# Prologue of an attention and SoLU-FFN kernel: fewer warming products, five paired key tiles, another order in the first score tile

## The chip, the cores and the metric

The kernel runs on one core of a Trainium2 chip. The metric is the device time of one execution in microseconds (us), as the median of several executions. TensorE (PE) multiplies matrices, VectorE (DVE), ScalarE (ACT) and GpSimd (POOL) work on the elements, and the queue of SyncE (SP) issues most of the DMAs.

## What is computed

Attention over pooled keys, and behind it a feed-forward layer with the SoLU activation, for 4 batches of 12288 tokens with 128 channels:

```python
r = 4
kv_pool = kv.reshape(B, H // r, r, W // r, r, C).mean(axis=(2, 4))
kv_flat = kv_pool.reshape(B, -1, C) @ w_sr        # 768 keys of 128 channels; k = v = kv_flat
s = (q @ k.transpose(0, 2, 1)) / sqrt(C)
a = softmax(s)                                     # written out: max, exp, sum
x = a @ v
h = x @ w_in                                       # 128 -> 1024
solu = h * softmax(h)
ln = (solu - mean) / sqrt(var + 1e-06) * g_ln
out = ln @ w_out                                   # 1024 -> 128
```

The weights of the feed-forward layer come as 64-bit floats and are taken apart into 32-bit parts on the chip.

## The kernel before

Work goes in tiles of 128 tokens, 384 tiles in all. A loop of slots is software-pipelined: in each slot one tile's scores `s` are made (L590, six products of 128x384), an earlier tile's values `xa`, hidden layer `h` and output `o`. All four engines are near full in it. The order of every instruction is written out by hand; each engine takes its own instructions strictly in that order, and waits on semaphores between engines.

The change lies in the prologue, ahead of the loop. The pooled keys of batch 0 are made there from 16 tiles `kv_0` (`kv_first_load`, L184): 8 tiles `c` for each half of the keys, each of 128 x 2 x 384 floats (384 KB). `kv_first` multiplies both planes of a tile with `w_sr16` on TensorE in float32 (two instructions for one product) and adds the products up in `pk`, one `pk` for each half. For the tiles named in `PAIRS` `kv_pair` first adds the second plane to the first, so that one product is enough; the tiles of half 1 are multiplied in the order `TURN1`. The tiles are called "tile 0" to "tile 7" of their half below. Out of `pk` come `kwh` (ACT, L211) and the remainder `kwl` (DVE, L214), 384 columns for each half; the first score tile `s_0` needs both halves of both, and of the queries `qwh` (ACT) and `qwl` (`q_low`, POOL, L573). The loop begins with `s_0`: its row maximum `nm` (DVE, L611), the exponential (ACT), and so on.

Beside that, the prologue takes the weights apart. `out_steps` are the seven steps for `w_out` on DVE, of which step 5 is a two-input operation over 128x1024 (`top_out`) and step 6 another (`rest_out`). POOL then subtracts (`wf`, L955) and adds (`wo`, L956, which needs step 6). Ahead of all products stand `WARM` products of a constant (L910), which nothing reads.

SP's queue issues all loads of the prologue in order: `w_sr`, `raw_in`, six tiles of half 0, `raw_out`, two tiles of half 0, the queries, the eight tiles of half 1 in the order 0 to 7, more queries and the first six tiles of batch 1.

Of the kernel before, what the change touches and what calls it, by code (L numbers as in the profile page):

```python
# [18 lines left out]
ALU = mybir.AluOpType  # L19
# [30 lines left out]
LOW_DVE = [NT - 2]  # L50
ROOM = {NT - 9: (0, 0), NT - 8: (0, 1), NT - 7: (0, 2), NT - 3: (1, 0), NT - 2: (1, 1), NT - 1: (1, 2)}

PAIRS = (2, 5, 6)
TURN1 = (0, 1, 3, 2, 4, 5, 7, 6)
OUT_AT = 6
Q_AT = 8
WARM = 20

Z_LEAST = 0.5
FIT_LEAST = 32.0  # L60
# [8 lines left out]
def kernel(  # L69
# [15 lines left out]
    nc = tc.nc  # L85
# [22 lines left out]
    def float64_parts(raw, name):  # L108


        pair = raw.rearrange("p (f two) -> p f two", two=2)
        lo, hi = pair[:, :, 0], pair[:, :, 1]
        top = wrk.tile([P, DFF], F32, tag="u", name=f"top_{name}", bufs=5)
        if name == "in":
            rest = wrk.tile([P, DFF], F32, tag="u", name="rest_in", bufs=5)
        else:
            rest = bat.tile([P, 2 * NK], F32, tag="acc", name="rest_out", bufs=1)[:, :DFF]
        ex = wrk.tile([P, DFF], I32, tag="e", name=f"ex_{name}")
        sgn = wrk.tile([P, DFF], I32, tag="e", name=f"sgn_{name}")
        scalar = nc.vector.tensor_scalar  # L120
        both = nc.vector.tensor_tensor
        and_, shr = ALU.bitwise_and, ALU.logical_shift_right
        return top, rest, [
            partial(scalar, ex, hi, 20, 0x7FF, op0=shr, op1=and_),
            partial(scalar, ex, ex, -896.0, 0.0, op0=ALU.add, op1=ALU.max),
            partial(scalar, ex, ex, 255.0, 2.0**23, op0=ALU.min, op1=ALU.mult),
            partial(
                nc.vector.scalar_tensor_tensor,
                ex,
                hi,  # L130
                -0x80000000,
                ex,
                op0=and_,
                op1=ALU.bitwise_or,
            ),
            partial(scalar, sgn, hi, 0xFFFFF, 3, op0=and_, op1=ALU.logical_shift_left),
            partial(both, top.bitcast(I32), ex, sgn, op=ALU.bitwise_or),
            partial(
                nc.vector.scalar_tensor_tensor,
                rest,  # L140
                lo.bitcast(U32),
                2.0**-52,
                ex.bitcast(F32),
                op0=ALU.mult,
                op1=ALU.mult,
            ),
        ]
# [36 lines left out]
        nc.sync.dma_start(t, kv0[:, 2 * c : 2 * c + 2, half * 384 : half * 384 + 384])  # L184
        state["kv0", half, c] = t

    def kv_pair(c):
        t = state["kv0", 1, c]
        nc.gpsimd.tensor_tensor(t[:, 0, :], t[:, 0, :], t[:, 1, :], op=ALU.add)

    def kv_first(half, c):


        if c == 0:
            state["pk0", half] = (ps_x, ps_r)[half].tile(
                [P, 512], F32, tag="xr"[half], name=f"pk_0_{half}"
            )
        t = state.pop(("kv0", half, c))
        n = 1 if half and c in PAIRS else 2
        last = TURN1[-1] if half else 7  # L200
        for r in range(n):
            nc.tensor.matmul(
                state["pk0", half][:, :384],
                w_sr16,
                t[:, r, :],
                start=c + r == 0,
                stop=c == last and r == n - 1,
            )
# [4 lines left out]
    def kv_first_l(half):  # L213
        nc.vector.scalar_tensor_tensor(  # L214
            half_of("kwl", 0, half),
            state["pk0", half][:, :384],
            SCALE,
            half_of("kwh", 0, half).bitcast(F32),
            op0=ALU.mult,
            op1=ALU.subtract,  # L220
        )
# [312 lines left out]
    def by_tile(a):  # L534
        return a.rearrange("p (t j) -> p j t", j=GT)

    def in_tiles(a):
        return a.rearrange("p (j t) -> p j t", j=GT)

    def wide(g):  # L540
        return g < GPB or g >= NG
# [9 lines left out]
    def q_split(g):  # L551
        if NG <= g < NG + GPB:
            return
        qf = state["qf", g // QL][:, (g % QL) * 512 : (g % QL + 1) * 512]
        if wide(g):
            qh = grp.tile([P, 512], F32R, tag="qwh", name=f"qwh_{g}")
            ql = grp.tile([P, 512], F32R, tag="qwl", name=f"qwl_{g}")
        else:
            qh = grp.tile([P, 512], F16, tag="qh", name=f"qh_{g}")
            ql = grp.tile([P, 512], F16, tag="ql", name=f"ql_{g}")  # L560
        if wide(g):
            nc.scalar.copy(in_tiles(qh), by_tile(qf))
        else:
            nc.scalar.copy(qh, qf)
        state["q", g] = (qh, ql)

    def q_low(g):
        if NG <= g < NG + GPB:
            return
        qf = state["qf", g // QL][:, (g % QL) * 512 : (g % QL + 1) * 512]  # L570
        qh, ql = state["q", g]
        if wide(g):
            nc.gpsimd.tensor_tensor(  # L573
                in_tiles(ql), by_tile(qf), in_tiles(qh.bitcast(F32)), op=ALU.subtract
            )
        else:
            nc.gpsimd.tensor_tensor(ql, qf, qh, op=ALU.subtract)


    def scores_pe(t):  # L580
        g, j = divmod(t, GT)
        b = t // TPB
        qh, ql = state["q", g]
        names = ("kwh", "kwl") if wide(g) else ("kh", "kl")
        kh, kl = (state[n, b] for n in names)
        tokens = in_tiles if wide(g) else by_tile
        s = ps_r.tile([P, 2, 512], F32, tag="r", name=f"s_{t}")
        for n, (lh, rh) in enumerate(((qh, kh), (qh, kl), (ql, kh))):
            for half in range(2):
                nc.tensor.matmul(  # L590
                    s[:, half, :384],
                    tokens(lh)[:, j, :],
                    rh[:, half * 384 : (half + 1) * 384],
                    start=n == 0,
                    stop=n == 2,
                )
        state["s", t] = s[:, :, :384]
        state["free"] = s[:, :, 384:]

# [308 lines left out]
    warm = ps_o.tile([P, 512], F32, tag="o", name="warm")  # L908
    for _ in range(WARM):
        nc.tensor.matmul(  # L910
# [3 lines left out]
            start=True,  # L914
            stop=True,
# [16 lines left out]
    wo, wor, out_steps = float64_parts(raw_out, "out")  # L932
# [2 lines left out]
        f()  # L935
    pow2_under(wsc)
    nc.vector.tensor_scalar(wsc, wsc, 2.0**14, None, op0=ALU.mult)
    for f in out_steps[2:]:
        f()
    q_split(0)  # L940
    q_low(0)
    nc.scalar.mul(wf, wf, wsc)
    nc.scalar.copy(w_in_h, wf)
    nc.scalar.mul(wr, wr, wsc)
# [3 lines left out]
    kv_first_t(0)  # L948
    kv_sq(0, 0)
    kv_first_l(0)  # L950
    for c in PAIRS:
        kv_pair(c)
    for c in TURN1:
        kv_first(1, c)
    nc.gpsimd.tensor_tensor(wf, wf, w_in_h, op=ALU.subtract)  # L955
# [121 lines left out]
    held = []  # L1077
    q_load(2)
    scores_pe(0)
    scores_pe(1)  # L1080
    for slot in range(NT):
        i = slot - LH
# [19 lines left out]
        if slot != 8:  # L1102
            at(slot + 2 if slot < 8 else slot + 1, scores_pe)
# [188 lines left out]
    n = nc.values_load(count[0:1, 0:1], min_val=0, max_val=P)  # L1292
# [37 lines left out]
```

## Time and profile before

| | us |
|---|---|
| median of 3 executions | 1843.61 |
| lowest and highest | 1842.31, 1850.59 |
| profiled execution | 1841.4 |
| its span, first to last instruction | 1839.5 |
| busy: PE, DVE, ACT, POOL | 1818.2, 1768.4, 1749.2, 1665.6 |

The profile is that of one execution. Its span is counted from the first instruction; 1.9 us lie around it. Rows give the start, the length and the instruction with what it writes and reads; brackets behind a row name the idle time ahead of it and what ended that. A row that stands for several instructions (x20) has their whole stretch. Starts overlap the instruction before by up to a tenth of a microsecond.

### The profile page before, as it was taken

Reading aid. Unit: us, or ns where it says so; the run is one execution under the profiler, and the core shown is the slowest. Engines: PE = TensorE matmul, PEld = TensorE weight load, DVE = VectorE, ACT = ScalarE, POOL = GpSimd, SP = SyncE. Lnnn points to the kernel's source line nnn. Section 1 sums busy time; section 2 is a strip of 40 time slices with the busy share of each in tenths; the row PEclk is TensorE's granted clock in tenths of the full one; section 3 lists DMA queues with packets and bytes.
Section 4 is the critical chain, followed back from the end, with each engine's and each line's share of the span. In section 5 each row is a group of like instructions: output and inputs, shape, how many; then the busy total and the mean of one; then the engine's idle time right before and its main releaser. Section 6 shows DMA issues by size and latency. Waiting matters only on the chain.

```text
span 1839.5 us, 42799 instructions
## 1 busy us (share of the span) xinstructions
PE 1818.2 (99%) x15747; PEld 1216.9 (66%) x15747; DVE 1768.4 (96%) x2635; ACT 1749.2 (95%) x3129; POOL 1665.6 (91%) x1466
## 2 busy tenths in 40 slices
PE   8999999999999999999999999999999999999998
PEld 5577777777666666566666666666666666666666
DVE  6999999999999999999999999999999999999997
ACT  5999999999999999899999999999999999999997
POOL 5899999899999999889999999998988988888887
PEclk9999999999999999999999999999999999999999
DMA  8999999999999999999999999999999999999998
GB/s 301 202 243 241 237 242 242 237 230 231 250 230 250 250 233 234 225 245 235 235 244 249 236 243 248 244 233 221 233 240 231 222 230 229 235 227 236 223 226 170
DMA packets 1440026, 432.79 MB, mean 235 GB/s; under 512 B 1404608, under 2 KB 1408832, under 8 KB 1439552
## 3 DMA queue, kind: packets, MB, share of 16 engines
q1 hardware_dynamic: 1433616, 413.45, 111.3%
q10 hardware_dynamic: 6192, 16.52, 3.5%
q8 instruction: 126, 2.06, 0.5%
q14 instruction: 92, 0.75, 0.1%
HBM read 52.50 MB, written 25.17 MB: 42 GB/s over the span
## 4 chain that ended last, share of the span: by engine, by line
PE 82%; ACT 8%; DVE 3%; DMA 2%; issue 2%; POOL 2%; SPq 0%; DVEq 0%; POOLq 0%; ACTq 0%
PE o L831 24%; PE h L703 23%; PE s L590 18%; PE xa L650 17%; ACT e L727 2%; ACT junk L806 2%; ACT phl L614 2%; ACT s L612 1%; DMA uT<-uhl 1%; DMA kv<-in_kv_dram 1%; POOL uhl L765 1%; DVE junkd L711 1%; DVE nm L611 1%; POOL uhl L758 1%; DVE phl L622 1%
## 5 line engine op out<-in xcount | busy, mean ns | idle before, releaser
L765 POOL TENSOR_TENSOR uhl<-u,uhl 128x1024 f16<-128x1024 f32 x382 | 814.5, 2133 | 31.7
L831 PEld LDWEIGHTS <-uT 128*128 128x128 f16 x9072 | 537.2, 98 | 95.9 <-DMA uT<-uhl 9.6
L831 PE MATMUL o<-wch,uT 128*128 128x128 f16 x6048 | 568.2, 219 | 5.0 <-DMA uT<-uhl 4.8
L831 PE MATMUL o<-wcl,uT 128*128 128x128 f16 x3024 | 526.1, 219 | 0.0
L741 DVE SCALAR_TENSOR_TENSOR u<-h,rz,e 128x1024 f32<-128x1024 f32 x384 | 491.1, 1279 | 26.4 <-ACT e L727 18.9
L711 DVE TENSOR_SCALAR_CACHE_REDUCE junkd<-h,rz 128x1024 bf16<-128x1024 f32 x384 | 490.7, 1278 | 1.5 <-PE h L703 1.1
L758 POOL TENSOR_SCALAR uhl<-u 128x1024 f16<-128x1024 f32 x379 | 395.8, 1044 | 84.7 <-DVE u L741 76.4
L650 PE MATMUL xa<-pT,vhl 128*128 128x512 f16 x1728 | 469.8, 380 | 0.0
L727 ACT ACTIVATE e<-h,nm,rz 128x1024 f32<-128x1024 f32 x384 | 458.5, 1194 | 3.0 <-DVE junkd L711 3.0
L806 ACT ACTIVATE junk<-u,su 128x1024 bf16<-128x1024 f32 x384 | 438.0, 1141 | 0.1
L611 DVE TENSOR_REDUCE nm<-s 128x1 f32<-128x768 f32 x384 | 363.9, 948 | 16.8 <-PE s L590 13.1
L612 ACT ACTIVATE s<-s,nm 128x768 f32<-128x768 f32 x384 | 335.0, 872 | 41.1 <-DVE nm L611 40.9
L622 DVE SCALAR_TENSOR_TENSOR phl<-s,phl 128x768 f16<-128x768 f32 x384 | 365.6, 952 | 2.9 <-ACT phl L614 2.9
L614 ACT ACTIVATE phl<-s 128x768 f16<-128x768 f32 x384 | 311.1, 810 | 12.2
L703 PEld LDWEIGHTS <-xh 128*128 128x128 f16 x1536 | 141.0, 97 | 194.5 <-DVE phl L622 32.3
L650 PEld LDWEIGHTS <-vhl 128*128 128x128 f16 x1728 | 162.5, 98 | 135.5 <-issue 12.8
L703 PE MATMUL h<-w_in_h,xh 128*128 128x512 f16 x768 | 229.1, 380 | 1.6 <-DVE rz L685 1.0
L703 PE MATMUL h<-w_in_h,xl 128*128 128x512 f16 x768 | 228.5, 379 | 0.0
L703 PE MATMUL h<-w_in_l,xh 128*128 128x512 f16 x768 | 228.5, 379 | 0.0
L590 PEld LDWEIGHTS <-qh 128*128 128x128 f16 x1152 | 124.2, 113 | 43.7 <-issue 0.7
L590 PE MATMUL s<-kh,qh 128*128 128x384 f16 x576 | 140.6, 326 | 0.6 <-DVE u L741 0.6
L590 PE MATMUL s<-kh,ql 128*128 128x384 f16 x576 | 140.9, 326 | 0.0
(153 smaller groups left out, 1816.8 us busy)
## 6 DMA issues: line engine op xcount, KB each, us to landing
qf<-in_q_dram SPq DMA_DIRECT2D x96, 256.0 KB, 3.6
out_dram<-ob SPq DMA_DIRECT2D x96, 256.0 KB, 2.7
kv<-in_kv_dram ACTq DMA_DIRECT2D x42, 384.0 KB, 4.4
kv<-in_kv_dram SPq DMA_DIRECT2D x22, 384.0 KB, 7.5
pT<-phl SPq DMA_TRANSPOSE x384, 4.0
uT<-uhl SPq DMA_TRANSPOSE x378, 4.5
raw_in<-in_moe_w_in_dram SPq DMA_DIRECT2D x1, 1024.0 KB, 5.0
raw_out<-in_moe_w_out_dram SPq DMA_DIRECT2D x1, 1024.0 KB, 9.8
```

The lines of the kernel that those rows point to most:

```text
L590: nc.tensor.matmul(s[:, half, :384], tokens(lh)[:, j, :], rh[:, half * 384 : (half + 1) * 384], start=n == 0, stop=n == 2,)
L611: nc.vector.tensor_reduce(nm, s, axis=AX.XY, op=ALU.max, negate=True)
L622: nc.vector.scalar_tensor_tensor(phl[:, 1], state.pop(("s", t)), SC, phl[:, 0], op0=ALU.mult, op1=ALU.subtract)
L650: nc.tensor.matmul(xa, v[:, c, :], pT[:, :, a * NKC + c, :], start=n == 0, stop=n == len(seq) - 1)
L703: nc.tensor.matmul(h[:, hs], lh[:, ts], rh[:, hs], start=n == 0, stop=n == 2)
L711: nc.vector.tensor_scalar(junk, state["h", t], state["rz", g][1][:, j : j + 1], None, op0=ALU.mult, op1=ALU.min, accum_out=nm,)
L727: nc.scalar.activation(e, state["h", t], AF.Exp, bias=nm, scale=state["rz", g][0][:, js], accum_out=state["z2", g][:, js],)
L741: nc.vector.scalar_tensor_tensor(u, state.pop(("h", t)), state["rz", g][2][:, j : j + 1], state.pop(("e", t)), op0=ALU.mult, op1=ALU.mult, ...
L758: nc.gpsimd.tensor_scalar(uhl[:, 0, :], u, 1.0, 1.0, op0=ALU.mult, op1=ALU.mult)
L765: low.tensor_tensor(uhl[:, 1, :], u, uhl[:, 0, :], op=ALU.subtract)
L806: nc.scalar.activation(junk, u, AF.Square, scale=-float(DFF), bias=su, accum_out=state["v3", g][:, j : j + 1],)
L831: nc.tensor.matmul(po[:, ts], uT[:, a * NFC + c, :], w[:, c, :], start=start, stop=stop)
```

## The change

`WARM` goes from 20 to 15. `PAIRS` goes from tiles 2, 5, 6 to tiles 2, 3, 4, 5, 6 of half 1, and `kv_pair` takes an engine: POOL adds tiles 2 and 5, DVE adds 3, 4 and 6. The additions are issued earlier: POOL's tile 2 ahead of `q_low`, tile 5 behind it; DVE's tile 3 ahead of step 5 of `out_steps`, tile 4 behind that step, and tile 6 behind the first half's `kwl`, followed by step 6. `TURN1` is new. The first score tile makes the three terms of half 0 first, and of half 1 the two that need only `kwh` ahead of the one that needs `kwl`. Nothing is loaded otherwise.

```diff
-PAIRS = (2, 5, 6)
-TURN1 = (0, 1, 3, 2, 4, 5, 7, 6)
+PAIRS = (2, 3, 4, 5, 6)
+TURN1 = (0, 1, 2, 3, 4, 6, 5, 7)
-WARM = 20
+WARM = 15
-    def kv_pair(c):
+    def kv_pair(c, eng):
         t = state["kv0", 1, c]
-        nc.gpsimd.tensor_tensor(t[:, 0, :], t[:, 0, :], t[:, 1, :], op=ALU.add)
+        eng.tensor_tensor(t[:, 0, :], t[:, 0, :], t[:, 1, :], op=ALU.add)
-        for n, (lh, rh) in enumerate(((qh, kh), (qh, kl), (ql, kh))):
-            for half in range(2):
+        order = [(n, half) for n in range(3) for half in range(2)]
+        if t == 0:
+            order = [(0, 0), (1, 0), (2, 0), (0, 1), (2, 1), (1, 1)]
+        for at, (n, half) in enumerate(order):
...
-    for f in out_steps[2:]:
+    for f in out_steps[2:5]:
         f()
     q_split(0)
+    kv_pair(2, nc.gpsimd)
     q_low(0)
+    kv_pair(5, nc.gpsimd)
+    kv_pair(3, nc.vector)
+    out_steps[5]()
+    kv_pair(4, nc.vector)
...
     kv_first_l(0)
-    for c in PAIRS:
-        kv_pair(c)
+    kv_pair(6, nc.vector)
+    out_steps[6]()
     for c in TURN1:
         kv_first(1, c)
```

On DVE, from the last single-input step of `out_steps` to the remainder of half 1. In the names `kv_3_148` is tile 3 of half 1, `pk_0` and `pk_1` are the sums of the two halves. Before:

```order
L939 TENSOR_SCALAR sgn_out<-raw_out 128x1024
L939 TENSOR_TENSOR top_out<-ex_out,sgn_out 128x1024
L939 SCALAR_TENSOR_TENSOR rest_out<-raw_out,ex_out 128x1024
L214 SCALAR_TENSOR_TENSOR kwl_120<-pk_0_206,kwh_119 128x384
L214 SCALAR_TENSOR_TENSOR kwl_120<-pk_1_257,kwh_119 128x384
```

And now:

```order
L943 TENSOR_SCALAR sgn_out<-raw_out 128x1024
L189 TENSOR_TENSOR kv_3_148<-kv_3_148 128x384
L949 TENSOR_TENSOR top_out<-ex_out,sgn_out 128x1024
L189 TENSOR_TENSOR kv_4_150<-kv_4_150 128x384
L214 SCALAR_TENSOR_TENSOR kwl_120<-pk_0_201,kwh_119 128x384
L189 TENSOR_TENSOR kv_6_154<-kv_6_154 128x384
L961 SCALAR_TENSOR_TENSOR rest_out<-raw_out,ex_out 128x1024
L214 SCALAR_TENSOR_TENSOR kwl_120<-pk_1_254,kwh_119 128x384
```

Three additions, each on a tile that must have landed, stand between the steps.

On POOL, from the power for `wsc` to the addition for `wo`. Before:

```order
L931 TENSOR_TENSOR wsc<-wsc,mhalf 128x1
L573 TENSOR_TENSOR qwl_236<-qf_140,qwh_235 128x512
L189 TENSOR_TENSOR kv_2_146<-kv_2_146 128x384
L189 TENSOR_TENSOR kv_5_152<-kv_5_152 128x384
L189 TENSOR_TENSOR kv_6_154<-kv_6_154 128x384
L955 TENSOR_TENSOR top_in<-top_in,w_in_h 128x1024
L956 TENSOR_TENSOR top_out<-top_out,rest_out 128x1024
```

And now:

```order
L935 TENSOR_TENSOR wsc<-wsc,mhalf 128x1
L189 TENSOR_TENSOR kv_2_146<-kv_2_146 128x384
L573 TENSOR_TENSOR qwl_229<-qf_140,qwh_228 128x512
L189 TENSOR_TENSOR kv_5_152<-kv_5_152 128x384
L964 TENSOR_TENSOR top_in<-top_in,w_in_h 128x1024
L965 TENSOR_TENSOR top_out<-top_out,rest_out 128x1024
```

Tile 6 is gone from POOL, and tile 2 stands ahead of `q_low`, so `q_low` now stands behind the landing of tile 2.

On PE, the products of half 1. Before:

```order
L202 MATMUL pk_1_257<-kv_0_142,w_sr_93 128x384 x2
L202 MATMUL pk_1_257<-kv_1_144,w_sr_93 128x384 x2
L202 MATMUL pk_1_257<-kv_3_148,w_sr_93 128x384 x2
L202 MATMUL pk_1_257<-kv_2_146,w_sr_93 128x384
L202 MATMUL pk_1_257<-kv_4_150,w_sr_93 128x384 x2
L202 MATMUL pk_1_257<-kv_5_152,w_sr_93 128x384
L202 MATMUL pk_1_257<-kv_7_156,w_sr_93 128x384 x2
L202 MATMUL pk_1_257<-kv_6_154,w_sr_93 128x384
```

And now:

```order
L202 MATMUL pk_1_254<-kv_0_142,w_sr_93 128x384 x2
L202 MATMUL pk_1_254<-kv_1_144,w_sr_93 128x384 x2
L202 MATMUL pk_1_254<-kv_2_146,w_sr_93 128x384
L202 MATMUL pk_1_254<-kv_3_148,w_sr_93 128x384
L202 MATMUL pk_1_254<-kv_4_150,w_sr_93 128x384
L202 MATMUL pk_1_254<-kv_6_154,w_sr_93 128x384
L202 MATMUL pk_1_254<-kv_5_152,w_sr_93 128x384
L202 MATMUL pk_1_254<-kv_7_156,w_sr_93 128x384 x2
```

Tiles 3 and 4 are down to one product, and tile 7, which lands last, closes the half.

## Rows read from the trace of the kernel before

**Rows 1.** The page's span and busy times: busy us (share of the span) xinstructions.

```profile
span 1839.5 us, 42799 instructions
PE 1818.2 (99%) x15747; PEld 1216.9 (66%) x15747; DVE 1768.4 (96%) x2635; ACT 1749.2 (95%) x3129; POOL 1665.6 (91%) x1466
```

**Rows 2.** PE's waits from 75 us on: us in total, times, longest; the largest.

```profile
PE o L831 <- DMA uT<-uhl: 4.8, 5, 2.1
```

**Rows 3.** The chain that ended last, first 36 us: start, length, what.

```profile
12.61 8.98 DMA kv<-in_kv_dram
...
21.64 6.17 PE pk L202 x18
...
27.82 0.50 ACT kwh L211
...
28.37 1.40 PE s L590 x5
...
29.79 0.97 DVE nm L611
```

**Rows 4.** PE's weight loads in order of time, one for each matmul instruction.

```profile
5.86 0.15 PEld L910 LDWEIGHTS <-ones 128*128 128x128 bf16 x1 [0.28 <-issue]
6.17 1.39 PEld L910 LDWEIGHTS <-ones 128*128 128x128 bf16 x7 [0.17 <-issue]
7.68 4.92 PEld L202 LDWEIGHTS pk<-kv,w_sr 128*128 128x128 f32 x16
...
16.04 2.23 PEld L202 LDWEIGHTS pk<-kv,w_sr 128*128 128x128 f32 x8 [0.42 <-DMA kv<-in_kv_dram]
18.66 2.23 PEld L202 LDWEIGHTS pk<-kv,w_sr 128*128 128x128 f32 x8 [0.39 <-DMA kv<-in_kv_dram]
21.64 0.94 PEld L202 LDWEIGHTS pk<-kv,w_sr 128*128 128x128 f32 x4 [0.74 <-DMA kv<-in_kv_dram]
22.75 1.76 PEld L202 LDWEIGHTS pk<-kv,w_sr 128*128 128x128 f32 x6 [0.17 <-POOL kv L189]
...
25.58 1.59 PEld L202 LDWEIGHTS pk<-kv,w_sr 128*128 128x128 f32 x6 [0.42 <-DMA kv<-in_kv_dram]
```

**Rows 5.** PE in order of time, behind its longest wait after the start.

```profile
33.75 0.58 PE L590 MATMUL s<-kwh,qwh 128*128 128x384 f32 x2 [1.69 <-DVE sv L104]
```

**Rows 6.** DVE in order of time, 18 to 29 us.

```profile
18.65 0.69 DVE L939 TENSOR_SCALAR sgn_out<-raw_out 128x1024 int32<-128x1024 int32 x1
19.37 2.47 DVE L939 TENSOR_TENSOR top_out<-ex_out,sgn_out 128x1024 int32<-128x1024 int32 x1
21.76 2.02 DVE L939 SCALAR_TENSOR_TENSOR rest_out<-raw_out,ex_out 128x1024 f32<-128x1024 uint32 x1
23.70 0.55 DVE L214 SCALAR_TENSOR_TENSOR kwl<-pk,kwh 128x384 fp32r<-128x384 f32 x1
28.35 0.56 DVE L214 SCALAR_TENSOR_TENSOR kwl<-pk,kwh 128x384 fp32r<-128x384 f32 x1 [4.10 <-ACT kwh L211]
```

**Rows 7.** POOL in order of time, 18 to 36 us.

```profile
18.93 1.82 POOL L573 TENSOR_TENSOR qwl<-qf,qwh 128x512 fp32r<-128x512 f32 x1 [2.43 <-ACT qwh L562]
20.71 1.99 POOL L189 TENSOR_TENSOR kv<-kv 128x384 f32<-128x384 f32 x1
23.60 2.02 POOL L189 TENSOR_TENSOR kv<-kv 128x384 f32<-128x384 f32 x2 [0.91 <-DMA kv<-in_kv_dram]
25.58 2.12 POOL L955 TENSOR_TENSOR top_in<-top_in,w_in_h 128x1024 f32<-128x1024 f32 x1
27.66 2.38 POOL L956 TENSOR_TENSOR top_out<-top_out,rest_out 128x1024 f32<-128x1024 f32 x1
...
35.44 1.53 POOL L573 TENSOR_TENSOR qwl<-qf,qwh 128x512 fp32r<-128x512 f32 x1 [0.82 <-ACT qwh L562]
```

**Rows 8.** DVE's groups by shape: busy us, mean ns, the same operations for `w_in`.

```profile
L921 DVE TENSOR_TENSOR top_in<-ex_in,sgn_in 128x1024 int32<-128x1024 int32 x1 | 1.2, 1226 | 0.0
...
L921 DVE SCALAR_TENSOR_TENSOR rest_in<-raw_in,ex_in 128x1024 f32<-128x1024 uint32 x1 | 1.2, 1217 | 0.0
```

More of the change, by code (lines that the diff above doesn't have):

```diff
@@ L587, in scores_pe @@
         s = ps_r.tile([P, 2, 512], F32, tag="r", name=f"s_{t}")
-        for n, (lh, rh) in enumerate(((qh, kh), (qh, kl), (ql, kh))):
-            for half in range(2):
[L590 to L596, printed above, removed]
+        terms = ((qh, kh), (qh, kl), (ql, kh))
+        order = [(n, half) for n in range(3) for half in range(2)]
+        if t == 0:
+            order = [(0, 0), (1, 0), (2, 0), (0, 1), (2, 1), (1, 1)]
+        for at, (n, half) in enumerate(order):
+            lh, rh = terms[n]
+            nc.tensor.matmul(
+                s[:, half, :384],
+                tokens(lh)[:, j, :],
+                rh[:, half * 384 : (half + 1) * 384],
+                start=n == 0,
+                stop=(at == 2 or at == 5) if t == 0 else n == 2,
+            )
         state["s", t] = s[:, :, :384]
```

## Prediction

> **What bounds the kernel now.** I read the page first: PE is busy 99% of the span, the others 91 to 96% [rows 1]. From 75 us on PE's largest wait sums to 4.8 us [rows 2]. So in the loop PE sets the pace and gives nothing back: what the prologue gains or loses until the loop starts should reach the end whole. The loop starts with the row maximum of the first score tile, at 29.79 us. The question is when that instruction starts after the change; I call that the start of the loop.
>
> The chain shows what made it 29.79 [rows 3]: a load of a key tile that landed at 21.59, eighteen matmul instructions that end at 27.80, then `kwh`, then the score tile. The weight loads tell which tiles these are [rows 4]. Before 16.04, 18.66, 21.64 and 25.58 PE waited for a DMA. Four weight loads behind 21.64 are the two products of tile 3, six behind 22.75 are tiles 2 and 4, six behind 25.58 are tiles 7 and 6. So tile 3 lands at 21.59 and tile 7 at 25.54. Four tiles in 3.95 us are 0.98 each: tile 2 lands at about 20.61, tile 4 at 22.58, tile 5 at 23.57 (POOL waits for it until 23.60 [rows 7]) and tile 6 at 24.55. The change touches no load, so these landings stay. They are a floor: after 25.54 two products of tile 7 remain in any order.
>
> A float32 matmul instruction takes 6.17 / 18 = 0.343 us, a product two of them. From 25.58 six take 2.06, and the sum ends at 27.80, so 0.16 is added at the end.
>
> **Fewer warming products.** The warming products stand 0.43 apart until 5.86 and 0.2 apart after it [rows 4]: 512 columns in 0.43 us are the lower of the two clock levels (1.2 GHz), later it is the upper. The five that go are at the upper level, 1.0 us. But the first key product starts at 7.68 right behind the warming, and PE waits for landings at 16.04 and 18.66. What starts earlier waits longer there. I count zero; the bounds are zero and, if a gap ahead of the first tile cost something, the 0.42 us of slack at 16.04 covers it.
>
> **Fewer key products.** Tiles 3 and 4 each save one product, 0.69 us, but ahead of the last landing, where PE had time (0.42 us of waiting at 25.58). What counts is the tail: behind tile 7's landing six instructions become four, if tile 6 has been multiplied by then. That would end the sum at 25.58 + 4 x 0.343 + 0.16 = 27.11, 0.69 earlier.
>
> **The first score tile.** Before, it started its maximum 1.99 us after the end of the sum (29.79 - 27.80): `kwh` 0.5, then five instructions in 1.40, among them those on `kwl`, which ended at 28.91 [rows 3, 6]. Now the three terms of half 0 run under `kwh`; behind `kwl` (end of sum + 1.10) only one instruction is left, 0.17, plus 0.2 to the maximum: about 1.52. That saves 0.47. DVE's `kwl` must not be late for it.
>
> **The additions.** This is where I expect the change to fail. What does an addition on DVE cost beside POOL? Step 5 took 2.47 us beside POOL, its twin for `w_in` 1.23 with POOL idle; step 6 took 2.02 against 1.22 [rows 6, 8]. On POOL the first addition took 1.99, the others 1.01; `q_low` took 1.82, and 1.53 later [rows 7]. Now put the ends beside each other: `q_low` (POOL) ends at 20.75, step 5 (DVE) at 21.84, tile 2's addition (POOL) at 22.70, step 6 (DVE) at 23.78. The differences are 1.09, 0.86 and 1.08, each the instruction's own undisturbed length less 0.14. So the engines did not run slowly side by side; they took turns, each waiting for the whole of the other's instruction. `kwl` at 23.70 took 0.55 beside POOL's next addition: it reads only one operand from SBUF (the other is PSUM), and took no turn.
>
> The Trainium skill, SBUF — State Buffer, section "Who interferes with whom", says the same of the hold: a DVE instruction with two SBUF inputs and a GpSimd instruction that reads SBUF lock each other out for a whole instruction. Read as bandwidth sharing, the same overlap would give the third rival's sum, 1 us less; the row of `q_low`, 1.82 and not some 2.6, speaks for the rule.
>
> So I play the turns through. DVE ends `sgn_out` at 19.34 and now waits for tile 3's landing, 2.3 us in which it formerly did step 5. A 384-column addition on DVE I price at 0.55 alone (as `kwl`, the same columns), 0.41 behind a turn; bounds 0.41 and 0.95.
> - POOL adds tile 2 from 20.65 to 21.66.
> - DVE adds tile 3 from 21.63 to 22.18.
> - POOL's `q_low`, waiting: 22.18 + 1.53 - 0.14 = 23.57.
> - DVE's step 5: 23.57 + 1.09 = 24.66.
> - POOL's tile 5: 24.66 + 0.87 = 25.53.
> - DVE's tile 4: 25.53 + 0.41 = 25.94, then `kwl` of half 0 to 26.45, no turn needed.
> - POOL, behind tile 5, goes straight on to the subtraction for `wf`, 2.12 long: 25.94 + 1.98 = 27.92.
> - DVE's tile 6 stands behind that: 27.92 + 0.41 = 28.33.
>
> PE, waiting for tile 6 ahead of 5 and 7, then has eight instructions: 28.38 + 8 x 0.343 + 0.16 = 31.28. Step 6 on DVE runs from 28.3 to 29.5 (POOL's next addition waits for it), so `kwl` of half 1 is not late. The loop starts at 31.28 + 1.52 = 32.80.
>
> **The sum.** 32.80 - 29.79 = +3.0 us: the tail saves 0.47 in the score tile, and the end of the sum comes 3.48 later. POOL ends its addition for `wo` near 31.9, against 30.04, still ahead of the squares it needs next, so nothing else is late. On the profiled execution, 1841.4, that makes 1844.4; the median of the runs lies 2.2 above it, and 1843.6 + 3.0 = 1846.6.
>
> **Rivals.** First, **the cover holds**: no turns on these additions. Then tile 3 is ready at 22.18, step 5 ends at 23.4, tile 4 at 23.95, `kwl` at 24.5, tile 6 at 25.05; PE ends the sum at 25.1 + 2.74 + 0.16 = 28.0, and the loop starts at 29.5, 0.3 earlier; at the floor of 27.11 it would be 28.6, 1.2 earlier. 1842.4 to 1843.3, no slower than before. Against it speak the four ends above; for it, that DVE's additions are short.
>
> Second, **the clock falls**. In the play PE has nothing from about 23.0 to 26.0 and from 26.7 to 28.4. The longest such wait in the trace after the start is 1.69 us, and the instructions behind it still ran at the upper level [rows 5]; a wait of 3 us is not in it. If the clock falls to 1.2 GHz there, eight key instructions take 2.7 us more and the first score tile 1.0 to 1.7 (six instructions, two of which lie within 0.58 [rows 5], overlapping): by the lower 3.0 + 3.7 = +6.7, or 1850.3. It gets beyond 0.5% (9.2 us, 1852.8), about what a measurement here tells from no change, if the low level also holds for two or three more score tiles.
>
> Third, **sharing at half speed**: tile 3 at 22.6, step 5 at 24.9, tile 4 at 25.85, `kwl` at 26.4, tile 6 at 27.35, sum at 30.3, loop at 31.8: +2.0, 1845.6.
>
> Fourth, **POOL wins a turn**: if its subtraction comes ahead of tile 4 too, tile 6 ends 0.6 later: 1847.2.
>
> **How the numbers follow.** Turns as played 0.55, POOL wins 0.08, sharing 0.10, cover holds 0.13, clock falls 0.14. The likeliest gives 1846.6. The executions before spread from 1842.3 to 1850.6, so each case carries about 1.5 us. The range takes in the cover's lower end and the fallen clock: 1841 to 1851, leaving out the ends of both. Nearly all of this is within 0.5% of 1843.6, so: faster 0.02, same 0.94, slower 0.04 (the clock staying low into the loop).
>
> **What would show it.** After: an idle DVE from 19.3 to 21.6; DVE's two-input additions longer than 0.55 and ending just behind POOL's rows; the subtraction for `wf` ahead of tile 6; PE waiting for DVE ahead of tile 6 at about 28.3; the first maximum near 32.8; the loop's waits as before. It is wrong if tile 6's addition ends before 25.6, or if the key products behind the wait take 0.69 each instruction. Should the additions be as played and the time still fall, the loop gave something back, against my first paragraph.

## The result, and the profile after

The changed kernel takes 1853.23 us, the median of 22 executions. The kernel before takes 1840.32, also of 22. The ratio, of means, is 1.006 (95% interval 1.0035 to 1.0085), means 11.0 ± 2.1 us apart: slower, by well over the 6.7 us that the second rival priced, and outside my range. Ratio and means leave out one execution of after, 1870.3, which counts as slow; with it the means lie 11.8 apart. The three executions shown before had put the old kernel at 1843.6. With 22 it is seen to spread from 1835.3 to 1857.6, the new one from 1841.0 to 1870.3. The lowest of each lie 5.8 apart, the means 11.0: there are two parts to explain, one that is always there and one that varies.

The page of after, against [rows 1]:

```profile
span 1853.0 us, 42786 instructions
PE 1821.8 (98%) x15738; PEld 1218.1 (66%) x15738; DVE 1771.6 (96%) x2638; ACT 1749.9 (94%) x3129; POOL 1665.7 (90%) x1465
```

PE is busy 3.6 us longer with nine instructions fewer, so some ran slower, and it is idle for 31.2 us against 21.3.

**The prologue.** DVE of after in order of time (start, length, line, operation, tiles, idle time ahead and its releaser), against [rows 6]:

```profile
18.41 0.69 DVE L943 TENSOR_SCALAR sgn_out<-raw_out 128x1024 int32<-128x1024 int32 x1
21.39 0.56 DVE L189 TENSOR_TENSOR kv<-kv 128x384 f32<-128x384 f32 x1 [2.29 <-DMA kv<-in_kv_dram]
21.86 2.56 DVE L949 TENSOR_TENSOR top_out<-ex_out,sgn_out 128x1024 int32<-128x1024 int32 x1
24.34 1.34 DVE L189 TENSOR_TENSOR kv<-kv 128x384 f32<-128x384 f32 x1
25.61 0.54 DVE L214 SCALAR_TENSOR_TENSOR kwl<-pk,kwh 128x384 fp32r<-128x384 f32 x1
26.08 2.01 DVE L189 TENSOR_TENSOR kv<-kv 128x384 f32<-128x384 f32 x1
28.01 1.21 DVE L961 SCALAR_TENSOR_TENSOR rest_out<-raw_out,ex_out 128x1024 f32<-128x1024 uint32 x1
...
34.18 0.56 DVE L214 SCALAR_TENSOR_TENSOR kwl<-pk,kwh 128x384 fp32r<-128x384 f32 x1 [4.96 <-ACT kwh L211]
35.28 2.00 DVE L615 TENSOR_REDUCE nm<-s 128x1 f32<-128x768 f32 x2 [0.54 <-PE s L594]
```

POOL of after, the same columns, against [rows 7]:

```profile
20.45 1.00 POOL L189 TENSOR_TENSOR kv<-kv 128x384 f32<-128x384 f32 x1 [4.19 <-DMA kv<-in_kv_dram]
21.40 1.94 POOL L573 TENSOR_TENSOR qwl<-qf,qwh 128x512 fp32r<-128x512 f32 x1
23.37 1.91 POOL L189 TENSOR_TENSOR kv<-kv 128x384 f32<-128x384 f32 x1
25.23 2.44 POOL L964 TENSOR_TENSOR top_in<-top_in,w_in_h 128x1024 f32<-128x1024 f32 x1
```

Read the two side by side, by their ends: tile 2 at 21.45 (POOL), tile 3 at 21.95 (DVE), `q_low` at 23.34 (POOL), step 5 at 24.42 (DVE), tile 5 at 25.28 (POOL), tile 4 at 25.68 (DVE), the subtraction for `wf` at 27.67 (POOL), tile 6 at 28.09 (DVE). Eight turns, strictly alternating between the two engines. One 384-column addition costs DVE 0.56, 1.34 or 2.01 us by what POOL is doing. `kwl`, which reads one operand from PSUM, takes 0.54 beside POOL.

PE of after, the same columns, and then the granted clock by stretch (busy us and instructions of PE, PEld, DVE, ACT, POOL; granted clock; DMA share; GB/s):

```profile
21.50 1.56 PE L202 MATMUL pk<-kv,w_sr 128*128 128x384 f32 x4 [0.24 <-POOL kv L189]
25.74 0.91 PE L202 MATMUL pk<-kv,w_sr 128*128 128x384 f32 x2 [2.68 <-DVE kv L189]
28.14 5.48 PE L202 MATMUL pk<-kv,w_sr 128*128 128x384 f32 x8 [1.49 <-DVE kv L189]
...
39.24 0.59 PE L594 MATMUL s<-kwh,qwh 128*128 128x384 f32 x2 [1.69 <-DVE sv L104]
```

```profile
18.00:26.60 8.60, 5.68 (x16) 2.43 (x15) 6.32 (x7) 5.11 (x8) 6.12 (x4) 1.00 1.06 405
26.65:33.45 6.80, 5.31 (x10) 2.89 (x10) 2.57 (x2) 0.00 (x0) 3.36 (x2) 0.50 0.73 291
33.50:40.00 6.50, 4.76 (x25) 3.85 (x24) 4.30 (x7) 5.26 (x11) 3.27 (x6) 1.00 0.00 0
```

PE waits 2.68 and then 1.49 us for DVE, with one product between, and the granted clock falls to 0.50 (1.2 GHz) from 26.65 to 33.45. The eight key instructions take 5.48 where the same eight take 2.85 at the upper level (a_fill, below). The loop starts at 35.28, against 29.79 [rows 3]: +5.5.

**The loop.** PE's largest wait from 75 us on (us in total, times, longest), against [rows 2]:

```profile
PE o L835 <- DMA uT<-uhl: 10.7, 11, 2.2
```

It was 4.8. Two pieces of the chain of after, which ended last (start, length, what), and the queues of SP and of ACT there (start, length of the issue):

```profile
222.38 8.60 DMA uT<-uhl
231.03 2.39 PE o L835 x24
```

```profile
222.38 1.78 SPq L784 DMA_TRANSPOSE uT<-uhl  x1
224.22 0.57 SPq L531 DMA_DIRECT2D qf<-in_q_dram  x1
224.90 5.47 SPq L629 DMA_TRANSPOSE pT<-phl  x1
230.46 2.34 SPq L784 DMA_TRANSPOSE uT<-uhl  x1
```

```profile
223.00 0.36 ACTq L230 DMA_DIRECT2D kv<-in_kv_dram  x1
```

ACT's queue issued a load of a key tile, 384 KB, at 223.00, and SP's a load of queries, 256 KB, at 224.22. The transpose of 222.38 lands 8.6 us after its issue, the next one blocks SP for 5.47 (1.43 is usual), and PE waits 2.15 and then runs at the lower clock:

```profile
231.03 0.23 PE L835 MATMUL o<-wch,uT 128*128 128x128 f16 x1 [2.15 <-DMA uT<-uhl]
```

```profile
231.45:234.85 3.40, 3.40 (x25) 3.31 (x23) 0.63 (x1) 1.54 (x4) 3.38 (x2) 0.50 1.61 282
```

The 24 products took 2.39 where the same 24 elsewhere in the chain take 1.51. Slot by slot against before's profile, the delay of the row maximum is 5.5 at the start, 6.5 ahead of this place, 10.4 at slot 48 behind it, and 13.5 at the end. So the loop adds, against what I wrote of it.

### The profile page after: what moved, and what is told of

Read it like the earlier page. It is cut to its first block, busy times and chain, and to the rows that moved or that the text cites. A ratio compares the mean times of both kernels' runs of the same rounds, so it can differ in the third digit from the quotient of the medians.

```text
span 1853.0 us, 42786 instructions
## 1 busy us (share of the span) xinstructions
PE 1821.8 (98%) x15738; PEld 1218.1 (66%) x15738; DVE 1771.6 (96%) x2638; ACT 1749.9 (94%) x3129; POOL 1665.7 (90%) x1465
## 4 chain that ended last, share of the span: by engine, by line
PE 65%; ACT 12%; DVE 8%; DMA 6%; issue 5%; POOL 4%; SPq 0%; DVEq 0%; POOLq 0%; ACTq 0%
PE o L835 19%; PE h L707 18%; PE s L594 14%; PE xa L654 13%; ACT e L731 3%; DMA uT<-uhl 3%; ACT junk L810 3%; ACT phl L618 3%; DVE junkd L715 2%; DVE nm L615 2%; ACT s L616 2%; DMA kv<-in_kv_dram 2%; POOL uhl L769 1%; DVE phl L626 1%; POOL uhl L762 1%
## 5 line engine op out<-in xcount | busy, mean ns | idle before, releaser
L594 PE MATMUL s<-kl,qh 128*128 128x384 f16 x576 | 140.6, 326 | 0.0
```

Source lines behind the costliest of these rows:

```text
L594: nc.tensor.matmul(s[:, half, :384], tokens(lh)[:, j, :], rh[:, half * 384 : (half + 1) * 384], start=n == 0, stop=(at == 2 or at == 5) if ...
```

## Experiments

Theories ahead of the first four: **A**, all of it is the prologue (turns and clock) and the loop only carries it on; **B**, a late start shifts the loop against its transfers, and any delay of that size costs more than itself; **C**, something else in the change disturbs the loop. The texts on record use letters of their own. In the first four, P is A and L is B. Later, C and C2 say that the place of the instructions decides, and N that it doesn't; S says that the excess belongs to the kernel, and R that it is chance or the chip's; A there says that the additions leave something behind; K is the theory D further down. "Start" below is the first row maximum against before's 29.79; "mean" is the mean of all executions against those of the kernel before in the same series of runs, with its standard error; "rest" is mean minus start.

**Fill PE's waits** (after, plus products of constants, 512 columns each, into a tile that nobody reads: twelve behind tile 3, six behind tile 4):

```diff
+    def fill_pe(n):
...
         kv_first(1, c)
+        fill_pe({3: 12, 4: 6}.get(c, 0))
```

> The changed kernel with 18 products of a constant into the unread tile put into PE's two waits: 12 behind the product of tile 3 and 6 behind that of tile 4. Theory P (the prologue is all that the change costs: turns between DVE and POOL, then the clock): the clock record stays at its upper level, the eight instructions behind tile 6 take 2.8 us and not 5.5, the loop starts at 32.8 and not 35.3, and the time is that of the kernel before plus 3.2. Theory L (a late or slow start costs the loop more as well): the same start, but the time is 5 to 9 us above before.

Measured: ratio 1.0042 (1.0016 to 1.0067), start +3.0, mean +7.1 ± 1.8. PE and its clock, and the first maximum:

```profile
23.08 2.75 PE L924 MATMUL warm<-ones 128*128 128x512 bf16 x12
25.91 0.91 PE L202 MATMUL pk<-kv,w_sr 128*128 128x384 f32 x2
26.66 1.46 PE L924 MATMUL warm<-ones 128*128 128x512 bf16 x6
28.31 2.85 PE L202 MATMUL pk<-kv,w_sr 128*128 128x384 f32 x8 [0.19 <-DVE kv L189]
```

```profile
26.65:33.45 6.80, 6.55 (x26) 3.89 (x25) 3.94 (x4) 1.59 (x4) 3.55 (x2) 1.00 0.76 301
```

```profile
32.81 2.00 DVE L615 TENSOR_REDUCE nm<-s 128x1 f32<-128x768 f32 x2 [0.53 <-PE s L594]
```

The clock stays at 1.00 and the eight instructions take 2.85: the fallen clock is worth 2.5 us of the start. The other 3.0 are the turns, less the 0.3 that the score tile gains (b_warm_s0, below). The loop begins at 32.81; the play of turns had said 32.80. The rest, 4.1 us, is still there.

**A late start alone** (before, plus 28 such products ahead of the first score tile):

```diff
+    def fill_pe(n):
...
+    fill_pe(28)
```

> The kernel before with 28 products of a constant between its last key product and the first score tile, 28 x 0.213 = 6.0 us of a busy PE: the loop starts at 35, as in the changed kernel, without an addition on DVE and without a lower clock. Theory P: 5.4 us above before, and the waits of the loop as before. Theory L, if it is the late start alone: 11 to 13 us above before, as the changed kernel.

Measured: 1.0045 (1.0024 to 1.0067), start +4.9, mean +5.7 ± 1.5; rest 0.8. The first row maximum:

```profile
34.73 0.96 DVE L611 TENSOR_REDUCE nm<-s 128x1 f32<-128x768 f32 x1 [6.02 <-PE s L590]
```

Theory B falls: a delay costs about itself.

**Undo DVE's wait** (after, steps 5 and 6 ahead of the additions):

```diff
-    for f in out_steps[2:5]:
+    for f in out_steps[2:]:
...
-    out_steps[5]()
...
-    out_steps[6]()
```

> The changed kernel with steps 5 and 6 of the weights put back ahead of DVE's additions (the additions of tiles 3 and 4 then follow, tile 6 behind kwl). By turns: step 6 ends at 21.4, tile 3 at 22.6, q_low at 24.0, tile 4 at 24.4, tile 6 at 25.7, the sum at 28.7, the loop starts at 30.2; PE waits at most 1.6 us, so the clock stays. Theory P: 0.7 us above before. If the additions themselves and not their place behind DVE's wait are what is late, the loop starts at 33 or later.

Measured: 1.0049 (1.002 to 1.0079), start +0.95 (0.5 later than expected), mean +8.0 ± 2.0. DVE:

```profile
20.61 1.22 DVE L943 SCALAR_TENSOR_TENSOR rest_out<-raw_out,ex_out 128x1024 f32<-128x1024 uint32 x1
21.86 3.04 DVE L189 TENSOR_TENSOR kv<-kv 128x384 f32<-128x384 f32 x2
...
30.74 2.00 DVE L615 TENSOR_REDUCE nm<-s 128x1 f32<-128x768 f32 x2 [0.53 <-PE s L594]
```

The step no longer waits for POOL and takes 1.22. So 4.5 of the 5.5 hang on DVE standing idle for tile 3's landing with the steps behind it, the clock's 2.5 among them, since PE's waits there are under 1 us. But the rest is 7.1 ± 2.0 us: the loop's part does not hang on the late start.

**Warming and first score tile alone** (before):

```diff
-WARM = 20
+WARM = 15
...
+        if t == 0:
+            order = [(0, 0), (1, 0), (2, 0), (0, 1), (2, 1), (1, 1)]
```

> The kernel before with 15 warming products and the new order in the first score tile, and nothing of the additions. The warming saves nothing, since PE waits for landings at 16.0 and 18.6; the score tile starts the loop 0.4 to 0.5 us earlier, at 29.3. Theory P: 0.4 us under before, not to be told from it by the runs. If the reordered score tile or the shorter warming were what costs the loop its time, 5 us or more above before.

Measured: 0.9998 (0.9968 to 1.0029), start −0.28, mean −0.1 ± 1.8. Both parts are harmless; the new order is worth 0.3, not the 0.47 of my working.

Theory A falls too: a_fill and a_steps_first keep a rest that a start doesn't explain. What is left of C is DVE's three added instructions, by themselves or by shifting all the instructions behind them. The next runs put instructions in or out without any work, or one addition alone: three tiny memsets in before (b_pad3), 40 of them (b_pad40), 37 in after (a_pad37);

```diff
+    for _ in range(3):
+        nc.vector.memset(mhalf[:, 0:1], -0.5)
```

> The kernel before with three one-column constants written again on DVE while it waits for the first weights (1.3 to 6.2 us): DVE's stream is three instructions longer, as the changed kernel's is, and nothing else moves; the loop starts at 29.7. Theory C (the loop of the changed kernel waits more because DVE's stream of instructions lies three further on against the loop): 4 to 6 us above before. Theory N (the position of the stream means nothing): within 2 us of before.

> As the run with three, with forty: about 3 us of DVE's wait are filled, the loop starts at 29.7. Theory C: a time of its own, which may lie some us above or at before, since the stream lies elsewhere. Theory N: within 2 us of before.

three constants (`mhalf`, `ones16`, `onesm`) written by POOL and not DVE, in after (a_pool_consts) and in a_fill (a_fill_pool_consts);

```diff
-    nc.vector.memset(mhalf, -0.5)
+    nc.gpsimd.memset(mhalf, -0.5)
...
```

> The changed kernel with the 18 filling products and with its three constants written by POOL instead of DVE, so that DVE's stream is as long as before; POOL's is three longer. The loop starts at 32.7 as with the filling products alone. Theory C: 3 us above before, the excess of the loop gone. Theory N: 7 us above before, as with the filling products alone.

and, in before, the addition of tile 6 alone on DVE (b_dve6):

```diff
+    def kv_pair(c, eng=None):
...
-    for c in PAIRS:
-        kv_pair(c)
+    kv_pair(2)
+    kv_pair(5)
+    kv_pair(6, nc.vector)
```

> The kernel before with the addition of tile 6 alone moved from POOL to DVE, behind the first kwl, in the old order of the products. DVE is idle there: the addition takes its turn behind POOL's tile 5, 24.6 to 25.0, before tile 7 lands, and nothing waits for it; the loop starts at 29.7. Turns theory: within 1 us of before. If an addition on DVE costs the loop time wherever it stands: 3 us or more above before.

A series on another chip repeated four kernels, and the last four of these ran in one more series:

> The changed kernel unchanged, beside the three that follow on one chip. Its loop starts 5.5 us later than before's. Theory S (the loop's excess belongs to this kernel): 10 to 12 us above before again. Theory R (the excess is chance or the chip's): 5 to 7 us above before.

> The changed kernel with the 18 filling products, again, on this chip. Loop start 3.0 us later than before's. Theory S: 7 us above before, as the first time. Theory R: 2 to 5 us.

> The same with the three constants written by POOL, again. Loop start 2.7 us later than before's. It had no excess the first time, on another chip than the one that showed the excess. Theory S with DVE's stream as the cause: 2.7 us above before, and the run with filling products alone 4 us above this one. Theory R: both within 2.5 us of each other.

> The kernel before with 28 products that delay the loop's start by 5.0 us, again. Both theories: 5 to 6 us above before; under theory S it lies 5 us under the changed kernel, under theory R within 2.5 us of it.

> The changed kernel with its three constants written by POOL instead of DVE, and nothing else: DVE's stream is as long as before. Loop start 5.5 us later than before's. Theory C2 (the place of the instruction streams against the loop decides how often the loop waits, whatever the additions do): 5 to 6 us above before, the excess gone. Theory A (the additions leave something behind that costs the loop): 10 to 12 us above before.

> The changed kernel with 37 one-column constants written again on DVE in its first wait. Loop start 5.5 us later than before's. Theory C2: an excess of its own, between 0 and 8 us beyond 5.5. Theory A: 10 to 12 us above before.

> The kernel before with the addition of tile 6 on DVE, again, on this chip; the loop starts 0.1 us earlier than before's. Theory C2 and theory A both allow the 4 us above before that the first runs showed; chance would bring it within 2 us of before.

> The kernel before with forty one-column constants on DVE, again. There is no addition on DVE and the loop starts with before's. Theory C2: 3 us above before, as the first time. Theory A, or chance the first time: within 2 us of before.

| kernel | ratio (95%) | start | mean ± s.e. | rest |
|---|---|---|---|---|
| b_pad3 | 0.9997 (0.9974–1.002) | −0.1 | −0.1 ± 1.7 | 0.0 |
| b_pad40 | 1.0012 (0.9985–1.0039) | −0.1 | +3.0 ± 2.1 | 3.1 |
| b_pad40_again | 1.0024 (1.0004–1.0044) | 0.0 | +2.3 ± 1.7 | 2.3 |
| b_dve6 | 1.0017 (0.9993–1.0041) | −0.1 | +4.3 ± 1.8 | 4.4 |
| b_dve6_again | 1.0009 (0.9983–1.0034) | +0.1 | +1.6 ± 1.9 | 1.5 |
| a_fill_pool_consts | 1.0005 (0.9986–1.0024) | +2.7 | +2.6 ± 1.3 | −0.1 |
| a_fill_pool_consts_again | 1.0017 (0.999–1.0043) | +2.8 | +3.0 ± 1.6 | 0.2 |
| a_pool_consts | 1.0046 (1.002–1.0072) | +5.3 | +8.1 ± 1.9 | 2.8 |
| a_pad37 | 1.0038 (1.0011–1.0064) | +5.0 | +6.6 ± 1.9 | 1.6 |
| after_again | 1.0064 (1.0033–1.0095) | +5.6 | +11.5 ± 2.5 | 5.9 |
| a_fill_again | 1.0036 (1.0017–1.0056) | +2.8 | +6.8 ± 1.9 | 4.0 |
| b_late_again | 1.0031 (1.0011–1.0052) | +4.7 | +4.8 ± 1.6 | 0.1 |

The rest of after (5.5, 5.9) and of a_fill (4.1, 4.0) came back on another chip, so it belongs to the kernels. With three constants written by another engine it is not seen in a_fill, in either series: the means differ by 4.5 ± 2.2 and 3.7 ± 2.2. In after it is smaller with that edit or with 37 empty instructions, but by no more than the noise. These edits do no work in the loop; what they move is where DVE's (and POOL's) later instructions stand. That points to placement, but doesn't show it: b_pad3 shifts DVE by the same three instructions and costs nothing, b_pad40 lies 3.0 ± 2.1 and 2.3 ± 1.7 up (of the two intervals only the second lies above no change), and b_dve6 gave 4.4 once and 1.5 the other time. Nor do loads of instructions explain the one stall shown. They have DMA queues of their own on the page, and between 222.4 and 231 us of after only two queues moved anything (queue and kind, packets, MB, share of 16 engines), SP's with the transposes and the query load, and ACT's with the key load:

```profile
q1 hardware_dynamic: 3602, 1.11, 83.4%
q10 hardware_dynamic: 144, 0.39, 32.8%
```

**Halve the loop's key loads.** The other end of the chain could be tried directly. Theory D: the rest is waiting on transposes that meet a 384 KB load; with the loads in two halves, two slots apart, it should go in either kernel, wherever the code lies. All outputs are computed as before.

```diff
...
-            yield load, [partial(kv_load, b, pos)]
+            for half in range(2):
+                yield load + 2 * half, [partial(kv_load, b, pos, half=half)]
```

> The kernel before with each of the 42 key loads of the loop (384 KB, issued on ACT) issued as two of 192 KB, two slots apart; nothing else moves, the loop starts at 29.7. In the traces so far the loop's longer waits of PE begin in the slot behind such a load. Theory K (a load in the middle of the transposes makes SP's queue late, and PE waits for the transposed tile): the waits get fewer, the mean of the executions falls by 3 to 6 us, towards the fastest executions of before (1835). If the loads only happen to stand there: within 2 us of before.

> The changed kernel with the same split loads. Loop start 5.5 us later than before's. Theory K: the excess of the loop goes with the waits, 1840 to 1843, that is within 7 us above the kernel before with split loads and at or under the kernel before. Otherwise 10 to 12 us above before, as without the split.

Measured, against a before of 1843.88 in the same series of runs: b_split 1839.71, ratio 0.9989 (0.9972 to 1.0005), mean −2.7 ± 1.2; a_split 1845.19, 1.0009 (0.9996 to 1.0023), mean +1.5 ± 0.9, though its loop starts 4.9 late. PE's wait on the transposes from 75 us on, of a_split and then b_split:

```profile
PE o L841 <- DMA uT<-uhl: 1.2, 2, 0.9
```

```profile
PE o L837 <- DMA uT<-uhl: 4.3, 6, 1.5
```

One profile of each decides nothing: b_split's 4.3 is hardly less than the 4.8 of before [rows 2]. But the executions of the changed kernel draw together: their standard deviation is 1.8 us in a_split, 7.5 in after and 8.0 in after_again. For b_split that can't be said: 3.2, and 3.4 of before in the same series. a_split minus b_split is 4.2 ± 1.1 us of mean, 5.0 of start: with the loads halved the change costs its prologue and no more, where with whole loads it cost 11.0 ± 2.1. The changed kernel with whole loads was not in this series, so that comparison goes across chips. Both levels fell a little short of what was expected: b_split gained 2.7 and not 3 to 6, and a_split lies 1.5 above before and not at it. (The halving adds 42 loads to ACT's instructions, so it moves code too.)

That the part that varies is PE's wait on `uT`, the 20 profiles show together. The time of each execution, less the start of its loop, lies within 2.5 us of 1805.7 plus 1.47 times that wait (correlation 0.98), from 1806.7 with no such wait (a_fill_pool_consts) to 1828.7 with 14.0 us (a_fill_again). Kernels made from before and from after lie on the same line.

The issues of SP's transposes in all profiles, 75 to 1500 us, worked out from the rows of SP's queue, show the transposes slowed beside these loads. An issue's row begins only when the instruction that makes its input has ended, in every case, so its length holds no wait for that; "beside" is issued within 5 us after a key load's issue:

| transpose | loads | issues beside a load | mean us, over 4 us | issues elsewhere | mean us, over 4 us |
|---|---|---|---|---|---|
| `uT` | whole, 18 profiles | 673 | 3.65, 31% | 4810 | 2.32, 0.5% |
| `uT` | halved, 2 profiles | 163 | 2.68, 1.8% | 449 | 2.32, 0.2% |
| `pT` | whole, 18 profiles | 595 | 1.88, 5.0% | 4887 | 1.55, 0% |
| `pT` | halved, 2 profiles | 163 | 1.85, 0.6% | 449 | 1.55, 0% |

A `uT` transpose that SP issues beside a whole load on ACT's queue holds SP for over 4 us in a third of the cases, and practically never elsewhere. Two things limit what that says; both are counted from the same rows.

First, key loads and query loads go out in the same slots: all whole key loads lie within 6 us of a query load on SP's own queue, and all but 12 of the 673 issues stand within 5 us behind a query load too. Behind a query load alone 1.3% of 679 are over 4 us; beside half a key load and a query load, 2 of 81. So the long holds belong to both loads meeting, and halving one ends them. No run moved one away from the other.

Second, most of the long holds cost PE nothing. Of 738 whole key loads 208 have one beside them, and PE waits for `uT` in the 15 us behind only 18 of these 208. PE's waits go with another thing, that SP's queue runs behind ACT's: 262 key loads go out over 0.5 us ahead of their query load, and 74 of them have such a wait, 99 us in sum of 109 in all. Of the other 476, 7 have one, 3 us in sum. With halved loads the same lag comes at 38 loads, and 2 have a wait.

So D holds this far: the part that varies is PE's wait for transposes behind a key load, and with halved loads the changed kernel is rid of it. What stays open is why after pays more for this than before, with the same 42 loads in the same slots. SP lags at 16 loads in after's profile and at 12 in before's, but at 14 in that of a_fill_pool_consts, which has no wait.

b_split has the lowest median of its series, but its interval takes in no change, so I don't call it faster.

## Why the prediction was wrong, point by point

- **The floor and the landings** stood: tiles 2 and 3 landed when I had played them, within 0.3 us.
- **Warming at zero, score tile −0.47**: b_warm_s0 shows the first, and 0.3 for the second.
- **The turns**, my main term: right. All eight came in the order played, tile 6 at 28.09 (played 28.33), and a_fill starts its loop at 32.81 (played 32.80). That it fits to 0.01 is luck: the sum ended 0.12 earlier than played, and the score tile took 0.13 longer. Sharing, the cover that holds and POOL's extra turn are all refuted by the same rows. The Trainium skill's rule on the lock (SBUF — State Buffer, "Who interferes with whom") agrees with the trace: 2.01 us for an addition that takes 0.56 alone. The row of `q_low` in [rows 7] fits a turn as well, but behind the one-input `sgn_out` [rows 6]: 19.34 + 1.53 − 0.14 = 20.73, and it ends at 20.75. So one-input steps may hold POOL too; no run tried it.
- **The clock**, second rival, chance 0.14: this is what happened, and the step that failed first. My sum took the eight key instructions behind the waits at 0.343 us each; they took 0.685, the sign of being wrong that I had named. I saw the waits of about 3.0 and 1.7 us in my own play, and weighed them by the row where 1.69 did no harm [rows 5]. That row was no evidence for longer ones, and little for its own length: the same wait stands in all 20 profiles, and in four of them the clock falls behind it. The low clock is in all five profiles of the changed kernel with unfilled waits, and in none of the four with filled ones; a_fill shows 2.5 us for it. The price (+3.7) was too high by 1.2: the key instructions took +2.6 (priced 2.7), but the clock came back at 33.45, so the first score tile kept little of its +1.0. The forecast should have been this rival.
- **"What the prologue loses reaches the end whole"**, the first paragraph: failed, and it is the larger error. The loop of after adds 5.5 us (5.9 in after_again) to the start's 5.5, in waits for transposes that I had expected "as before". I took [rows 2] as a property of the loop, but it is one execution's. The executions before already spread over 8 us with nothing changed, which a loop that only follows PE's pace would not do; I put 1.5 us on each case for it and asked no further.
- **The base**: 1843.6 from three executions was 3.3 above what 22 give. Starting from 1840.3 the second rival would have said 1847.0, and the range would have been 3 us lower still, away from the result.
- **Within 0.5%**: the median lies 0.7% up, the means 0.6%, and the interval straddles 0.5%. The chance of 0.04 for slower rested on the low clock reaching into the loop; the loop's part came with PE's waits on the transposes.

## What to carry to other kernels

Before putting two-input VectorE work beside GpSimd, play the turns by whole instructions, and don't let a VectorE instruction that waits for a landing stand ahead of steps that are ready: here that cost 4.5 us. If the play leaves TensorE waits longer than any the trace has, price the lower clock in, or fill them: eighteen idle products won back 2.5 us of the loop's start here. And where executions of one kernel spread by several us, find the wait that varies before calling the loop rigid: here it was worth as much as the whole delay of the prologue.

## What the runs showed of the hardware

- The clock fell behind waits of 2.68 and 1.49 us with 0.9 us of work between, and behind one of 2.15 in the loop; each time it was low for several us (6.8, 3.4). In a_pad37 and a_split it had fallen before the first of these waits ended. After a wait of 1.66 to 1.69 it stayed up in 16 profiles (after's row 39.24 among them), and fell in b_late (granted 0.54 from 38.7 to 42 us), a_pad37, a_split and a_fill_pool_consts_again. What makes the difference I did not settle.
- A key load of 384 KB on ACT's queue and a query load on SP's, issued together, go with slow transposes on SP's: issues of `uT` over 4 us in 31%, and in 1.8% beside key loads of 192 KB. PE paid for it where the key load went out over 0.5 us ahead of the query load: 74 of 262 such loads, against 7 of the other 476.
- The mean of a kernel seems to move by some 4 us when instructions that do no work in the loop are put elsewhere (a_fill against a_fill_pool_consts: 4.5 ± 2.2 and 3.7 ± 2.2). That is not far outside the noise, and the mechanism is open.
